# A third addition in chunks 1 to 4, one load moved ahead of another, and a new written order

## The chip, the cores and the metric

The kernel runs on one core of a Trainium2 chip. The metric is device time in microseconds (us). The time before is the median of three runs. A profile is one further execution that the hardware profiler recorded; its times count from the first instruction.

The core has five instruction queues that run side by side: PE (TensorE, matrix multiplication; its weight loads are shown as PEld), DVE (VectorE), ACT (ScalarE), POOL (GpSimd) and SP (SyncE, which here only starts transfers). Each works through its own list in order and waits for others through semaphores. Matmuls write to PSUM, which is used here as eight banks.

## The reference

Linear attention, then a feed-forward layer with SoLU and a layer norm. Cut to what matters:

```python
# q, k, v: (8 batches, 8 heads, 576 rows, 64)
kv  = einsum('bhsd,bhse->bhde', k, v)
o   = einsum('bhsd,bhde->bhse', q, kv)
x   = o / sqrt(mean(o*o, -1) + 1e-6) * g_norm     # then to 4608 rows x 512
h   = x @ w_in                                    # 512 x 1024
e   = exp(h - max(h))
u   = h * e / (sum(e) + 1e-9)                     # over the 1024 columns
ln  = (u - mean(u)) / sqrt(var(u) + 1e-6) * g_ln
out = ln @ w_out                                  # 1024 x 512
```

## The kernel before

The 4608 rows are worked in nine chunks of 512. Chunks 0 to 7 hold 512 of the 576 rows of one batch each; chunk 8 holds the other 64 rows of all eight. Everything between the matmuls lies transposed: features on partitions, the 512 rows of a chunk along the free axis.

The steps of a chunk c, with the names that the order uses (f counts eight groups of 128 features, m four groups of 128 rows, hf two halves of the heads, z the two members of a half):

- `k`, `v`, `q`, `q_last`, `w_in`, `w_out`: loads. They are issued from POOL; all but w_out are turned to bf16 on the way. The second half of chunk 0's k and v is loaded as f32 from SP (`wide`) and converted by `k.0.1` and `v.0.1`. In chunks 0 and 1 each of k, v, q comes in two halves.
- `kv_mm` (line 375): k^T v into PSUM, 72 small matmuls a chunk; `kv`: copies of the result to SBUF, in pieces (line 229).
- `qT`: q transposed, in chunks 0 to 3 by PE (`qT_mm`, line 427) with a copy, from chunk 4 on by a transposing transfer issued from SP.
- `o_mm` (line 448): q times kv. `sq`: squares of o (ACT, line 233). `oa`: the sum of the two squares (line 460). `s_mm` (line 465): the mean over a head. `ln`, `ex`: the inverse root. `x` (line 489): o scaled, on DVE.
- `h` (line 532): x times w_in, four matmuls a group; in chunks 0 to 2 in two parts, the first of which needs only x of the first half and `w_in.0`. `exp` (line 539, ACT) gives e. `u` (line 543, DVE) is h times e; it reads the PSUM bank of h and so sets when that comes free. `usq`: the square of u, on POOL or ACT. `es` (line 551, POOL): e added in pairs of groups, four rows of 512 a chunk.
- `ua.c.l`, `usqa.c.l`, `esa.c.l` (line 575, DVE): folds. Fold l adds the upper half of the groups to the lower, so that eight become four, two, one.
- `sums` (line 594): what the folds left is summed over the partitions by small matmuls, four for each row of 512. `turn`, `stats`, `rstd`: mean, variance and the inverse root.
- `out` (line 651): u times a centred w_out, eight matmuls for 128 rows; in parts of two matmuls in chunk 0, of four in the others. Chunk 8's last tile is done in two halves of 256 columns (line 659). `ob` (lines 239 and 241): the scaling, on DVE or ACT. `store`: two transfers from SP, in chunk 8 one from SP or ACT.
- `w_mean`, `w_center` (lines 632 and 638): the column mean of g_ln times w_out, once, by eight matmuls, and eight DVE instructions that centre w_out. `warm`: matmuls on zeros, as many as `WARM` says; their result is not used.

The sum's denominator and the variance are put together in `stats`; the maximum is not subtracted.

Nothing is scheduled by the compiler. `ORDER` is a list of all these steps, written out; each queue gets its steps in that order. A step runs on its default engine unless a suffix names another (`usq.0.5:act`, `oa.2.1:pool`; `usq` is on POOL, `oa`, `kv`, `ob`, folds are on DVE without a suffix). `ROOMS` names the buffer or PSUM bank that each new tile takes, so a step also waits until the former holder of its room has been read.

`Plan.run` (lines 122 to 139) adds waits beyond those of the data: the next POOL instruction waits for every DVE addition (`ua`, `usqa`, `esa`, `oa`) that stands ahead of it in the order, and POOL loads wait for a transposing transfer ahead of them.

`FOLDS` and `E_FOLDS` give the number of folds of u (and its square) and of e for each chunk. After two folds of u and none of e, `sums` has (2 + 2 + 4) x 4 = 32 matmuls; after three and one, (1 + 1 + 2) x 4 = 16; in chunk 0, without folds, (8 + 8 + 4) x 4 = 80.

Of the kernel before, what the change touches and what calls it, by code (L numbers as in the profile page):

```python
# [25 lines left out]
kv.1.0.0.0 kv.1.0.1.1 kv.1.0.1.0 qT_mm.1.0 ex.0.0 q.2.0 qT.1.0:act x.0.0.0 x.0.0.1 warm.5 o_mm.1.0 sq.1.0.0 warm.6
h.0.6.0 h.0.3.0 k.2.0 sq.1.0.1 x.0.1.0 table h.0.0.0 oa.1.0 x.0.1.1 s_mm.1.0 h.0.2.0 h.0.7.0 h.0.2.1 ln.1.0 v.2.0
ex.1.0 h.0.6.1 x.1.0.1 exp.0.6 q.3.0 h.0.3.1 exp.0.2 x.1.0.0 h.0.7.1 h.0.1.0 exp.0.7 u.0.6 v.3.0 qT_mm.1.1 h.0.0.1
exp.0.3 h.0.1.1 u.0.2 usq.0.6 h.1.2.0 exp.0.0 qT.1.1 kv_mm.1.1.1 exp.0.1 kv_mm.1.1.0 k.3.0 kv.1.1.0.1 h.0.4.0 h.0.4.1
u.0.1 kv.1.1.2.1:act kv.1.1.0.0:act es.0.0 kv.1.1.1.0:act kv.1.1.2.0:act kv.1.1.1.1 u.0.3 o_mm.1.1 exp.0.4 h.0.5.0  # L30
# [10 lines left out]
out.0.3.2 rstd.0 h.2.0.0 ob.0.0:act usq.1.6 kv.3.0.1 ob.0.2 h.2.6.1 kv.3.1.2:act kv.3.0.0:act kv.3.1.1:act out.0.3.3
usqa.1.0 kv.3.0.2:act h.2.4.0 exp.2.6 h.2.5.0 ob.0.3:act ua.1.0 o_mm.3.0 h.2.1.0 store.0.3 sq.3.0.0 h.2.0.1 sq.3.0.1
u.2.6 h.2.1.1 store.0.0 exp.2.0 h.2.5.1 usqa.1.1 out.0.1.0 exp.2.1 oa.3.0 h.2.4.1 ua.1.1 exp.2.5 qT.4 s_mm.3.0
out.0.1.1 u.2.0 ln.3.0 es.1.3 out.0.1.2 u.2.5 h.2.7.0 ex.3.0 h.2.7.1 u.2.1 exp.2.4 es.2.0 h.2.3.0 x.3.0.1 exp.2.7
o_mm.3.1 sq.3.1.0 x.3.0.0 usq.2.6 out.0.1.3 sq.3.1.1 h.2.2.0 h.2.3.1 u.2.7 qT.5 ob.0.1:act h.2.2.1 oa.3.1 sums.1
exp.2.3 u.2.4 es.2.3 kv_mm.4.0 exp.2.2 u.2.3 store.0.1 usq.2.5:act s_mm.3.1 turn.1 es.2.2 out.1.3.0 kv.4.1.0
kv.4.0.1:act ln.3.1 u.2.2 store.0.2 out.1.3.1 kv.4.0.0 usq.2.7 ex.3.1 stats.1 out.1.2.0 kv.4.0.2:act kv.4.1.1 kv.4.1.2
rstd.1 x.3.1.1 usq.2.0 o_mm.4.0 o_mm.4.1 ob.1.3 sq.4.0.1 out.1.0.0 usq.2.4 x.3.1.0 sq.4.0.0 store.1.3 out.1.2.1
sq.4.1.0 oa.4.0 ua.2.0 sq.4.1.1 s_mm.4.0 out.1.0.1 ln.4.0 oa.4.1 h.3.2.0 ex.4.0 ob.1.0 v.5.0 s_mm.4.1 x.4.0.0 h.3.7.0
k.5.0 ln.4.1 x.4.0.1 exp.3.2 es.2.1 h.3.3.0 ex.4.1 u.3.2 h.3.6.0 exp.3.3 ua.2.1 exp.3.7 h.3.5.0 x.4.1.0 u.3.3 v.6.0  # L50
# [685 lines left out]
```

## Time and profile before

| | |
|---|---|
| median of 3 runs | 177.4 us (177.29 to 177.53) |
| the profiled execution: span from the first to the last instruction | 175.8 us |
| its own time beyond the span | not on the page; median less span is 1.6 us |
| PE busy | 164.2 us (93%) |
| ACT busy | 152.1 us (86%) |
| DVE busy | 145.5 us (83%) |
| POOL busy | 99.8 us (57%) |
| chain that ended last | PE 75%, DVE 10%, ACT 5%, DMA 5% |
| granted TensorE clock | 1.000 |

Busy time of PE counts a 128x512 matmul as 379 ns, though a row of them starts one every 0.22 us; they overlap, so short pauses are hidden in it. "Idle before" is the time for which an engine stood still ahead of an instruction, with what ended it. In the chain of waits each step is followed back to what released it, or to the instruction before it on its engine.

### The profile page before, as it was taken

What the parts mean: (1) busy time and instruction counts of PE and PEld (TensorE: products, weight loads), DVE (VectorE), ACT (ScalarE), POOL (GpSimd) and SP (SyncE); (2) the same over time, 40 slices, a digit from 0 to 9 for tenths busy, and PEclk for the clock granted to TensorE, in tenths of its full rate; (3) what the DMA queues carried; (4) which work ended last, traced back from release to release, by engine and by line L of the source; (5) the groups of instructions that cost most, each with busy time, mean ns of one, the idle gap of its engine ahead of it and who ended that gap; (6) DMA issues with size and microseconds to landing.
All of it is one profiled execution on the core that took longest, in us unless ns stands there. A gap on an engine that the chain in (4) does not pass through costs nothing.

```text
span 175.8 us, 4843 instructions
## 1 busy us (share of the span) xinstructions
PE 164.2 (93%) x1913; PEld 80.3 (46%) x1938; DVE 145.5 (83%) x317; ACT 152.1 (86%) x273; POOL 99.8 (57%) x108
## 2 busy tenths in 40 slices
...
GB/s 179 218 203 214 206 275 373 209 208 208 208 210 210 218 210 129 127 206 235 205 183 259 150 52 193 156 73 93 195 206 105 5 118 126 2 60 93 196 213 159
DMA packets 34623, 30.27 MB, mean 172 GB/s; under 512 B 16288, under 2 KB 28328, under 8 KB 34600
## 3 DMA queue, kind: packets, MB, share of 16 engines
...
q10 hardware_dynamic: 432, 0.66, 1.0%
...
HBM read 32.51 MB, written 9.44 MB: 239 GB/s over the span
## 4 chain that ended last, share of the span: by engine, by line
PE 75%; DVE 10%; ACT 5%; DMA 5%; issue 2%; POOL 1%; POOLq 0%; DVEq 0%; ACTq 0%
PE h_ps L532 31%; PE out_ps L651 30%; DMA k_sb<-in_k_dram 5%; PE kv_ps L375 4%; PE o_ps L448 3%; DVE u_sb L543 3%; PE sum_ps L594 3%; PE s_ps L465 3%; DVE x_sb L489 2%; DVE w_out_sb L638 2%; ACT osq_sb L233 2%; DVE osq_sb L460 1%; PE out_ps L659 1%; ACT e_sb L539 1%; ACT kvd L229 1%
## 5 line engine op out<-in xcount | busy, mean ns | idle before, releaser
L532 PE MATMUL h_ps<-x_sb,w_in_sb 128*128 128x512 bf16 x280 | 68.0, 379 | 0.5
L651 PE MATMUL out_ps<-w_out_sb,u_sb 128*128 128x512 bf16 x266 | 65.2, 379 | 0.7 <-issue 0.3
L551 POOL TENSOR_TENSOR es_sb<-e_sb 128x512 bf16<-128x512 f32 x36 | 45.4, 1279 | 33.5 <-ACT e_sb L539 13.0
L539 ACT ACTIVATE e_sb<-h_ps,zero_t 128x512 f32<-128x512 f32 x72 | 46.2, 690 | 2.3 <-PE h_ps L532 1.7
L543 DVE TENSOR_TENSOR u_sb<-h_ps,e_sb 128x512 bf16<-128x512 f32 x72 | 46.6, 684 | 1.3 <-ACT e_sb L539 1.0
L532 PEld LDWEIGHTS <-w_in_sb 128*128 128x128 bf16 x288 | 27.3, 98 | 32.5 <-issue 1.3
L651 PEld LDWEIGHTS <-u_sb 128*128 128x128 bf16 x280 | 26.4, 98 | 31.6 <-issue 1.0
L233 ACT ACTIVATE usq_sb<-u_sb,zero_t 128x512 bf16<-128x512 bf16 x49 | 33.6, 718 | 0.0
L489 DVE SCALAR_TENSOR_TENSOR x_sb<-o_ps,g_sb,rst_sb 128x256 bf16<-128x256 f32 x72 | 30.2, 478 | 3.1 <-ACT rst_sb L476 2.5
L235 POOL TENSOR_TENSOR usq_sb<-u_sb 128x512 bf16<-128x512 bf16 x23 | 23.6, 1043 | 7.9 <-DVE osq_sb L460 5.6
L233 ACT ACTIVATE osq_sb<-o_ps,zero_t 128x512 bf16<-128x512 f32 x36 | 22.8, 689 | 3.5 <-PE o_ps L448 3.4
L239 ACT ACTIVATE ob_sb<-out_ps,rstd 128x512 f32<-128x512 f32 x22 | 14.8, 684 | 4.0 <-PE out_ps L651 3.8
L575 DVE TENSOR_TENSOR usq_sb<-usq_sb 128x2048 bf16<-128x2048 bf16 (+2 forms) x20 | 17.0, 848 | 0.6 <-ACT usq_sb L233 0.4
L229 DVE CAST kvd<-kv_ps 64x128 bf16<-64x128 f32 (+3 forms) x26 | 6.4, 256 | 11.2 <-ACT kvd L229 6.5
L241 DVE TENSOR_SCALAR ob_sb<-out_ps,rstd 128x512 f32<-128x512 f32 (+1 forms) x15 | 10.6, 711 | 4.1 <-PE out_ps L659 2.2
L322 POOL DMA_DIRECT2D v_sb<-in_v_dram x9 | 6.8, 757 | 10.1 <-DVE sum_ps L601 2.8
L472 ACT ACTIVATE lss_sb<-s_ps,eps_t 128x512 f32<-128x512 f32 x16 | 11.1, 695 | 1.0 <-PE s_ps L465 0.7
L476 ACT ACTIVATE rst_sb<-lss_sb,zero_t 128x512 f32<-128x512 f32 x16 | 11.5, 722 | 0.4
L375 PE MATMUL kv_ps<-v_sb,k_sb 64*64 64x64 bf16 x576 | 8.0, 194 | 2.8 <-DMA k_sb<-in_k_dram 1.3
L300 PE MATMUL warm_ps<-zeros 128*128 128x512 bf16 x25 | 8.8, 481 | 1.4 <-DVE zeros L255 1.2
L229 ACT CAST kvd<-kv_ps 64x128 bf16<-64x128 f32 (+3 forms) x34 | 8.2, 243 | 2.2 <-PE kv_ps L375 1.5
L375 PEld LDWEIGHTS <-k_sb 64*64 64x64 bf16 x576 | 6.8, 107 | 6.8 <-DMA k_sb<-in_k_dram 2.6
...
## 6 DMA issues: line engine op xcount, KB each, us to landing
...
k_sb<-in_k_dram POOLq DMA_DIRECT2D x6, 576.0 KB, 13.8
v_sb<-in_v_dram POOLq DMA_DIRECT2D x6, 576.0 KB, 13.0
q_sb<-in_q_dram POOLq DMA_DIRECT2D x6, 512.0 KB, 16.2
...
q_sb<-in_q_dram POOLq DMA_DIRECT2D x4, 256.0 KB, 9.9
w_in_sb<-in_moe_w_in_dram POOLq DMA_DIRECT2D x2, 512.0 KB, 13.4
...
```

The source lines that it names most:

```text
L229: nc.scalar.copy(dst, src) if engine == "act" else on[engine].tensor_copy(dst, src)
L233: nc.scalar.activation(out=dst, in_=src, func=AF.Square, bias=zero_t[:, :])
L235: on[engine].tensor_tensor(out=dst, in0=src, in1=src, op=MUL)
L239: nc.scalar.activation(out=dst, in_=src, func=AF.Copy, scale=by)
L375: nc.tensor.matmul(t[64 * y:64 * y + 64, :], T["k", b][rows, n, i, :], T["v", b][rows, n, i, :], start=(i == 0 and (b < 2 or m == 0)), sto ...
L489: nc.vector.scalar_tensor_tensor(out=t[:, 2 * hf + dh, z], in0=T["o", c, hf, z][:, dh], scalar=g_rep[dh], in1=T["rst", c, hf][:, z], op0=M ...
L532: nc.tensor.matmul(bank(("h", c, f), [128, 512])[:, :], w_in_sb[:, dt, f * 128:(f + 1) * 128], T["x", c][:, dt].rearrange("p a b c -> p (a ...
L539: nc.scalar.activation(out=t[:, f % 2, :], in_=T["h", c, f][:, :], func=AF.Exp, bias=zero_t[:, :])
L543: nc.vector.tensor_tensor(out=t[:, f, :], in0=T["h", c, f][:, :], in1=T["e", c, f // 2][:, f % 2, :], op=MUL)
L551: on[engine].tensor_tensor(out=t[:, n, :], in0=e[:, 0, :], in1=e[:, 1, :], op=ADD)
L575: nc.vector.tensor_tensor(out=to[:, 0:n, :], in0=src[:, 0:n, :], in1=src[:, n:2 * n, :], op=ADD)
L651: nc.tensor.matmul(bank(("out", c, m), [128, d_model])[:, :], T["u", c][:, f, m * 128:(m + 1) * 128], w_out_sb[:, f, :], start=(f == 0), s ...
```

## The change

1. `FOLDS` of chunks 1 to 4 goes from 2 to 3 and `E_FOLDS` from 0 to 1: the new steps are `ua.c.2`, `usqa.c.2` and `esa.c.0` for c from 1 to 4, all on DVE.
2. In POOL's list of loads `w_in.0` stands ahead of `q.1.0`; the order of all other loads is the same.
3. The order of everything else is written anew, with new rooms. Assignments move: on DVE, `ob` falls from 15 to 10, `oa` from 15 to 11, and `v.0.1` is added; on ACT, `ob` rises from 22 to 27 and `usq` falls from 49 to 46; on POOL, `usq` rises from 23 to 26 and `oa` from 1 to 5 (3.0, 4.1, 5.1, 8.0, 8.1 for 2.1). SP gains one store of chunk 8 that ACT had issued, and ACT scales both halves of the last tile.
4. There is an eighth `warm` step, and the warm-up matmuls are 42 instead of 27.

The diff, cut:

```diff
-wide.v ident wide.k g_rows q.0.1 v.0.0 k.0.0 q.0.0 v.0.1:act v.1.0 k.1.0 q.1.0 w_in.0 k.0.1:act w_in.1 warm.0
+ident wide.v v.0.1 wide.k g_rows k.0.1:act warm.0 kv_mm.0.1.1 kv_mm.0.1.0 kv.0.1.1.1:act q.0.1 qT_mm.0.1 qT.0.1:act
+turn_g v.0.0 k.0.0 q.0.0 warm.1 kv_mm.0.0.1 kv.0.0.2.1:act kv_mm.0.0.0 warm.2 qT_mm.0.0 kv.0.1.2.0:act v.1.0 k.1.0
 ...
+o_mm.0.1 w_in.0 q.1.0 qT.0.0 w_in.1 q.1.1 v.1.1 k.1.1 w_out.0 w_out.1 sq.0.1.1 q.2.0 warm.4 o_mm.0.0 sq.0.0.0 sq.0.0.1
 ...
-w_center.4 h.1.0.1 v.4.0 w_center.0 exp.1.7 qT_mm.2.0 exp.1.0 w_center.3 h.1.1.0 h.1.1.1 k.4.0 qT.2.0:act w_center.2
-h.1.2.1 es.0.1 u.1.7 h.1.3.1 exp.1.1 h.1.4.1 u.1.0 exp.1.3 out.0.2.0 es.1.0 usq.0.3 u.1.1 exp.1.2 out.0.2.1 kv_mm.2.0
-w_center.7 exp.1.4 h.1.5.0 w_center.6 kv.2.1.0:act kv.2.0.0:act h.1.5.1 kv.2.0.2:act kv.2.1.1 kv.2.0.1:act es.1.1
-u.1.4 out.0.2.2 kv.2.1.2:act exp.1.5 o_mm.2.0 u.1.3 o_mm.2.1 sq.2.0.1 out.0.2.3 usq.1.1 u.1.2 qT_mm.3.0 sq.2.0.0 u.1.5
-out.0.0.0 sq.2.1.1 oa.2.0 out.0.0.1 sq.2.1.0 qT.3.0 s_mm.2.0 usq.1.5 out.0.0.2 ln.2.0 qT_mm.3.1 oa.2.1:pool ex.2.0
 ...
+v.3.0 kv.1.0.1.0:act kv.1.0.0.0:act table g_mean x.0.0.1 x.0.0.0 kv.1.0.2.1:act warm.6 h.0.0.0 h.0.6.0 x.0.1.1 x.0.1.0
+kv.1.0.2.0 qT_mm.1.0 qT.1.0 h.0.3.0 h.0.4.0 o_mm.1.0 h.0.1.0 h.0.4.1 sq.1.0.0 h.0.1.1 sq.1.0.1 oa.1.0 h.0.6.1 exp.0.4
 ...
+h.0.2.0 exp.0.5 u.0.5 es.0.0 q.4.0 es.0.3 q.5.0 h.0.2.1 exp.0.2 es.0.1 es.0.2 w_mean.0 u.0.7 u.0.2 v.4.0 w_mean.1 k.4.0
+w_mean.2 w_mean.3 s_mm.1.1 ln.1.1 usq.0.6 ex.1.1 x.1.1.0 x.1.1.1 usq.0.7:act usq.0.0:act usq.0.2:act h.1.2.0 h.1.4.0
 ...
+h.1.7.1 qT_mm.2.0 exp.1.6 u.1.6 qT.2.0:act es.1.2 usq.1.0 sums.0 exp.1.7 u.1.7 kv_mm.2.0 kv.2.0.0:act kv.2.1.1:act
+turn.0 out.0.1.0 out.0.2.0 out.0.2.1 kv.2.0.1:act kv.2.1.2:act kv.2.0.2:act kv.2.1.0:act o_mm.2.0 usq.1.5:act
+w_center.6 stats.0 o_mm.2.1 w_center.7 out.0.1.1 out.0.1.2 sq.2.0.0 sq.2.0.1 oa.2.0 out.0.0.0 out.0.0.1 ua.1.0 sq.2.1.0
+sq.2.1.1 oa.2.1 s_mm.2.0 ln.2.0 es.1.1 out.0.1.3 out.0.2.2 out.0.2.3 out.0.0.2 out.0.0.3 s_mm.2.1 rstd.0 ex.2.0 ob.0.1
 ...
+es.3.0 usq.3.0 ua.3.0 sq.5.1.0 oa.5.1:pool exp.4.0 u.4.2 u.4.0 h.4.5.0 exp.4.5 sq.5.0.1 u.4.5 out.2.3.0 out.2.3.1
 ...
+stats.8 out.8.1.0 out.8.1.1 rstd.8 ob.8.0 ob.8.2:act store.7.1 store.8.2:act out.8.3.0 ob.8.3.0:act ob.8.1 store.8.0
+store.8.1 store.8.3.0 out.8.3.1 ob.8.3.1:act store.8.3.1:act
 ...
-14 3 1 3 1 4 1
+17 9 2 1 1 6 5 1
 ...
-    FOLDS = (0, 2, 2, 2, 2, 3, 3, 3, 3)
-    E_FOLDS = (0, 0, 0, 0, 0, 1, 1, 1, 1)
+    FOLDS = (0, 3, 3, 3, 3, 3, 3, 3, 3)
+    E_FOLDS = (0, 1, 1, 1, 1, 1, 1, 1, 1)
```

126 lines of the change are left out of this document (59 added, 67 removed).

## The prediction

> **What bounds the kernel now.** I read the page's head, then busy time by stretch, to find where PE (TensorE's matmul queue) is not full, then the timeline and the chain of waits in those places.
>
> ```profile
> span 175.8 us, 4843 instructions
> ...
> PE 164.2 (93%) x1913; PEld 80.3 (46%) x1938; DVE 145.5 (83%) x317; ACT 152.1 (86%) x273; POOL 99.8 (57%) x108
> ```
>
> The span is 175.8 us; the median of the runs shown is 177.4, so 1.6 us lie around the span. The page gives no other time of this execution, and I carry the 1.6 us unchanged: the sum is made on the span and added to 177.4.
>
> Busy time by stretch (columns: stretch, PE, PEld, DVE, ACT, POOL, granted clock, DMA share, GB/s):
>
> ```profile
> 20.00:30.00 10.00, 9.81 (x96) 4.66 (x96) 7.75 (x17) 9.61 (x18) 6.54 (x8) 1.00 1.21 305
> 30.00:45.00 15.00, 13.04 (x172) 7.17 (x174) 14.10 (x26) 13.75 (x26) 12.77 (x14) 1.00 1.22 211
> 45.00:50.00 5.00, 4.98 (x171) 3.25 (x171) 4.11 (x12) 4.51 (x8) 5.00 (x5) 1.00 1.23 207
> 50.00:160.00 110.00, 109.00 (x1189) 51.55 (x1204) 104.78 (x214) 105.58 (x192) 63.29 (x61) 1.00 0.80 146
> ```
>
> From 45 us on PE stands still for 1.0 us in 115, spread thin: there only less PE work, or a new wait, moves the end. Between 20 and 45 us it idles 0.19 + 1.96 = 2.15 us; this can be won back. ACT has 4.4 us free in the long stretch and DVE 5.2. The clock is 1.00 throughout, so more warm-up matmuls win no speed.
>
> The start, in the timeline and in the DMA issues with their time to landing:
>
> ```profile
> 6.07 0.75 POOL L322 DMA_DIRECT2D q_sb<-in_q_dram  x1
> 6.78 0.61 POOL L343 DMA_DIRECT2D w_in_sb<-in_moe_w_in_dram  x1
> 8.41 0.54 POOL L343 DMA_DIRECT2D w_in_sb<-in_moe_w_in_dram  x1 [1.03 <-DMA q_sb<-in_q_dram]
> ...
> 22.79 0.74 POOL L322 DMA_DIRECT2D v_sb<-in_v_dram  x1 [1.98 <-DMA w_in_sb<-in_moe_w_in_dram]
> ```
> ```profile
> 19.83 0.98 PEld L532 LDWEIGHTS <-w_in_sb 128*128 128x128 bf16 x6 [0.27 <-DMA w_in_sb<-in_moe_w_in_dram]
> ```
> ```profile
> w_in_sb<-in_moe_w_in_dram POOLq DMA_DIRECT2D x1, 512.0 KB, 13.0
> q_sb<-in_q_dram POOLq DMA_DIRECT2D x1, 256.0 KB, 11.3
> ```
> ```profile
> w_in_sb<-in_moe_w_in_dram POOLq DMA_DIRECT2D x1, 512.0 KB, 13.8
> ```
> ```profile
> v_sb<-in_v_dram POOLq DMA_DIRECT2D x1, 576.0 KB, 17.5
> ```
>
> Issue plus time to landing: q.1.0 is there at 17.4, w_in.0 at 19.8, w_in.1 at 22.2, chunk 2's v at 40.3. The loads arrive one behind the other, and the first h (line 532) waits for w_in.0.
>
> ```profile
> 26.60 0.76 PE L375 MATMUL kv_ps<-v_sb,k_sb 64*64 64x64 bf16 x36
> ...
> 31.08 0.38 PE L465 MATMUL s_ps<-osq_sb,head_mean 128*128 128x512 bf16 x1 [0.71 <-DVE osq_sb L460]
> 31.10 1.95 PE L632 MATMUL mean_ps<-u_sb,ua_sb 128*128 128x512 f32 x7
> ...
> 40.40 0.77 PE L375 MATMUL kv_ps<-v_sb,k_sb 64*64 64x64 bf16 x72 [0.51 <-DVE u_sb L543]
> ...
> 42.50 0.72 PE L448 MATMUL o_ps<-qT_sb,kvd 64*32 64x256 bf16 x32
> ...
> 44.92 0.38 PE L465 MATMUL s_ps<-osq_sb,head_mean 128*128 128x512 bf16 x1
> ```
>
> Three marks for later: kv_mm.2.0 starts at 40.40, o_mm.2.0 at 42.50, s_mm.2.0 at 44.92. No order can start kv_mm.2.0 before its v lands at 40.3.
>
> **The change part by part.** Prices of PE's pieces, from the chain of waits:
>
> ```profile
> 47.86 1.30 PE sum_ps L594 x80
> ...
> 61.53 0.56 PE sum_ps L594 x32
> ...
> 93.89 3.45 PE h_ps L532 x16
> ...
> 130.04 0.34 PE sum_ps L594 x16
> ```
>
> *Third folds.* In chunks 1 to 4 u and its square are added down to one row each instead of two, and e to two instead of four: sums has 16 small matmuls where it had 32, 0.34 for 0.56 us, four times: **-0.88 us** of PE work, all behind 45 us where PE is full. Without that cover it would be worth nothing.
>
> *What pays for it*, by shapes (count | busy us, mean ns of one | idle before, releaser):
>
> ```profile
> L233 ACT ACTIVATE usq_sb<-u_sb,zero_t 128x512 bf16<-128x512 bf16 x49 | 33.6, 718 | 0.0
> ...
> L235 POOL TENSOR_TENSOR usq_sb<-u_sb 128x512 bf16<-128x512 bf16 x23 | 23.6, 1043 | 7.9 <-DVE osq_sb L460 5.6 <-DVE usq_sb L575 2.2
> L233 ACT ACTIVATE osq_sb<-o_ps,zero_t 128x512 bf16<-128x512 f32 x36 | 22.8, 689 | 3.5 <-PE o_ps L448 3.4
> L239 ACT ACTIVATE ob_sb<-out_ps,rstd 128x512 f32<-128x512 f32 x22 | 14.8, 684 | 4.0 <-PE out_ps L651 3.8
> ...
> L241 DVE TENSOR_SCALAR ob_sb<-out_ps,rstd 128x512 f32<-128x512 f32 x13 | 9.6, 747 | 1.9 <-ACT rstd L617 1.0 <-PE out_ps L651 0.9
> ...
> L460 DVE TENSOR_TENSOR osq_sb<-osq_sb 128x512 bf16<-128x512 bf16 x15 | 6.7, 445 | 1.0 <-ACT osq_sb L233 0.6
> ...
> L575 DVE TENSOR_TENSOR es_sb<-es_sb 128x1024 bf16<-128x1024 bf16 x4 | 2.7, 685 | 0.0
> ...
> L229 ACT CAST kvd<-kv_ps 128x128 bf16<-128x128 f32 x8 | 2.0, 265 | 1.0 <-PE kv_ps L375 0.9
> ...
> L575 DVE TENSOR_TENSOR usq_sb<-usq_sb 128x512 bf16<-128x512 bf16 x4 | 1.7, 423 | 0.0
> L575 DVE TENSOR_TENSOR ua_sb<-ua_sb 128x512 bf16<-128x512 bf16 x4 | 1.7, 419 | 0.0
> ...
> L460 POOL TENSOR_TENSOR osq_sb<-osq_sb 128x512 bf16<-128x512 bf16 x1 | 1.1, 1150 | 0.0
> ```
>
> DVE gains 4 x (0.42 + 0.42 + 0.69) = 6.1 us and gives away four o additions (1.8) and five scalings (three whole ones 2.2, two halves under 1.5): about +1 us against 5.2 free. ACT takes those scalings (3 x 0.68, two halves at most as much) for three squares fewer (0.72 each): at most +1.3 us, taken as 1, against 4.4 free. POOL gets three squares (3.1) and four o additions (4.6), +7.7 us in a span where it works 57%. The conversion of v.0.1 moves from ACT to DVE in the first 8 us, while k.0.1's, which lands later, stays: 0. On average none becomes the bound: 0 us, from 0 up to the second rival. Plan.run makes the next POOL instruction wait for every DVE addition ahead of it in the order, so twelve folds are twelve such waits; behind them stand es and the loads of chunks 5 to 7. The order leaves 12.0 us of PE work between v.5.0 and its use (9.7 before), so I price them at 0; without that cover a late load stops PE for its whole delay.
>
> *The swap of w_in.0 and q.1.0.* w_in.0's turn lasted 2.4 us (17.4 to 19.8) and q.1.0 has half its bytes, so w_in.0 lands 1.2 to 2.4 us earlier, at 17.4 to 18.6, and q.1.0 near 19.8. The first h then waits for its x and five warm-up matmuls, somewhere from there to the old 19.8; I take 18.9. qT_mm.1.0 stands behind two h now, which hide the later q. But w_in.1 lands at 22.2 as before, and ahead of it both orders have issued ten h matmuls; before also had chunk 1's s_mm behind it, 0.2 us. Alone: **0 us**, bounds -0.9 (the earlier first h survives) and +0.5 (qT_mm.1.0 waits for q). Every other load keeps its place in POOL's queue, and SP's queue only gains one late store.
>
> *Warm-up matmuls.* 42 for 27; fourteen of the fifteen more stand before the first h, in waits for k and x; warm.7 is one h-sized matmul, 3.45 / 16 = 0.22 us, in front of a load, so 0 to 0.22, contained in the walk below.
>
> *The new order from 22.3 to 46 us*: the largest term. PE's list from h.0.4.1 to kv_mm.2.0 is 54 h matmuls (11.7 us), 8 w_mean (1.95 / 7 each: 2.2), three q transposes (about 0.5 each, between a kv group and its neighbours: 1.6), two 18-matmul kv groups (0.7), one o_mm (0.4), two s_mm (0.5), warm.7 and sums.0 (1.3): 18.6 us, so 40.9 without a wait. Waits I find by setting each piece against what it needs: kv_mm.1.1.0 not before 26.6 (its group started there; PE comes at 26.3), h.1.6.0 for the PSUM bank that ln.1.1 frees (0.1), crumbs 0.1. So **kv_mm.2.0 at 41.4, 1.0 us later** than before. But behind it 3.05 us less work is left: h.1.5 and h.1.6 (8 matmuls, 1.73) and sums.0 (1.30) moved ahead of it, the first two parts of out.0.2 (4 matmuls, 0.86) behind it, and the 0.88 of the folds. The w_center stall (0.51 for u in the row above) and the 0.71 at s_mm.1.1 do not return: s_mm.1.1 now stands behind h.0.2 and four w_mean.
>
> Late next is the copying of kv.2, all six pieces on ACT: 41.4 + 0.8 + 6 x 0.265 = 43.8, which puts o_mm.2.0 at 43.9 (PE is through with out.0.1.0 and out.0.2.0-1 at 43.6), and s_mm.2.0, behind o_mm.2 (0.72) and eight out matmuls (1.73), at 46.4, 1.5 later than before, with 3.03 us less PE work left. Sum at that mark: 1.48 - 3.03 = **-1.55 us**. The bounds of this term: kv_mm.2.0 right after its load and everything behind as before, -3.0; all 2.15 us of idle lost again, +0.6.
>
> *The tail.* The last half of the last tile is scaled on ACT instead of DVE and stored from the same queue; 0 us, plus or minus 0.2. sums.8 has 9.8 us of PE work between the last h and itself, 12.4 before; ACT and DVE work far below full there. 0, up to +1.
>
> The sum: 177.4 - 1.55 = **175.9 us**. It assumes that PE stays as full behind 46 us as before.
>
> **A rule against the change.** First the rows:
>
> ```profile
> 71.30 1.29 POOL L551 TENSOR_TENSOR es_sb<-e_sb 128x512 bf16<-128x512 f32 x1
> ...
> 72.29 0.85 DVE L575 TENSOR_TENSOR ua_sb<-ua_sb 128x1024 bf16<-128x1024 bf16 x1
> ```
>
> One fold began inside a POOL addition and ended 0.27 us behind it, in 0.85 us. The Trainium skill's page "SBUF — State Buffer", section "Who interferes with whom", says that a VectorE instruction with two SBUF inputs and a GpSimd instruction reading SBUF exclude each other for a whole instruction. By that rule each of twelve new folds may wait for what is left of a POOL addition; here that would have held this fold for up to 0.3 us. Its row agrees in part: 0.17 us above the 0.685 of the same shape.
>
> **The rivals.**
> 1. *PE is even better filled*: kv_mm.2.0 starts when its load lands. For: 2.15 us of idle are there, and all work before 40 us is free of that load. Against: my walk has 18.6 us of work in 18.1. 177.4 - 3.05, about 174.4.
> 2. *Slower: additions of o on POOL hold up s_mm.* One 1.15 us instruction for 0.445, behind whatever POOL is doing. From the order PE has 2.9 us of work from the second square to s_mm.5.1, 3.5 at chunk 8's two, 5.1 at chunks 3 and 4. Two squares (0.69 each), the addition and one POOL addition before it (1.29) are 3.8: waits of 0.9 and twice 0.3; with a POOL square (1.04) in front as well 2.0 and twice 1.4. Against: before, oa.2.1 ran on POOL unnoticed. At the upper price 175.9 + 4.8 = 180.7; halfway 179.0. It makes the kernel slower from 1.9 us in all, 0.6 at each of those three.
> 3. *No gain in the end*: PE asks 1.5 us earlier, but ACT and DVE, about 1 us fuller each, cannot deliver; 1.5 us are handed back in many small waits. For: 4.4 and 5.2 us of freedom shrink by 1 + 1.55 each. Against: they stay above 1.8. 177.4.
> 4. *Folds and POOL exclude each other*: a fold held for half a POOL addition, twelve times 0.64 = 7.7 us on DVE against 4 free: 175.9 + 3.7 = 179.6. The fold of 0.85 us speaks weakly for it.
>
> **How the numbers follow.** Forecast 0.56, rival 1 0.10, rival 2 0.14, rival 3 0.16, rival 4 0.04. The likeliest case alone spans 175.1 to 176.9 (a walk without its waits and crumbs below; half a microsecond of new waits and a late sums.8 above). The range reaches into rivals 1 and 3 and the light end of 2: 174.8 to 177.9. A measurement here tells 0.2% (0.35 us) from no change: faster 0.66, within 0.16, slower 0.18.
>
> **What would show it.** Right: the sums groups of chunks 1 to 4 as x16 at 0.34 us; first h near 18.9 without a gain at w_in.1; kv_mm.2.0 at 41.4, o_mm.2.0 at 43.9, s_mm.2.0 at 46.4; PE idle from 30 to 45 us about 1 us instead of 1.96; at most 1.2 us idle from 50 to 160. Wrong: s_mm waiting for POOL's osq in chunks 5 and 8 (rival 2); e or u ending many waits behind 50 us (3); folds of 128x512 far above 0.42 us (4); or kv_mm.2.0 at 43.4 instead of 41.4, which leaves nothing of the 3.05.

## The result and the profile after

| | before | after |
|---|---|---|
| median | 177.37 us (177.29 to 177.53) | 178.38 us (178.19 to 178.6) |
| after / before | | 1.0055, 95% interval 1.0041 to 1.0069 |
| span of the profiled execution | 175.8 us | 176.4 us (whole execution 178.19) |

The changed kernel is half a per cent slower; 175.9 had been forecast. In every later comparison the time beyond the span has a median of 1.8 us for the old and the new kernels alike, so the difference lies inside the span. The two profiled executions are 0.6 us apart, the medians 1.0: what is read from the two traces accounts for 0.6.

The page of the kernel after, its head and its chain by engine:

```profile
span 176.4 us, 4777 instructions
...
PE 166.4 (94%) x1864; PEld 80.8 (46%) x1889; DVE 148.8 (84%) x322; ACT 149.9 (85%) x273; POOL 107.5 (61%) x115
...
ACT 33%; PE 30%; DVE 25%; DMA 5%; issue 5%; SPq 0%; ACTq 0%; DVEq 0%
```

The chain that ended last was PE for 75% before. Now ACT and DVE hold 58% of it: PE does 0.9 us less of sums and yet ends later, because it waits for them in the places below.

Busy time by stretch (stretch, PE, PEld, DVE, ACT, POOL, clock, DMA share, GB/s), after:

```profile
30.00:45.00 15.00, 14.58 (x249) 8.51 (x250) 14.88 (x30) 14.63 (x28) 13.25 (x14) 1.00 1.22 210
...
50.00:100.00 50.00, 48.76 (x641) 22.95 (x649) 48.68 (x104) 48.88 (x91) 34.71 (x33) 1.00 0.98 189
100.00:150.00 50.00, 48.96 (x481) 22.64 (x486) 47.48 (x96) 47.45 (x85) 31.34 (x31) 1.00 0.72 122
```

The same view of the kernel before:

```profile
50.00:100.00 50.00, 49.47 (x629) 23.42 (x637) 48.10 (x99) 48.70 (x93) 31.25 (x30) 1.00 1.04 196
100.00:150.00 50.00, 49.63 (x504) 23.67 (x508) 46.79 (x97) 47.23 (x84) 27.84 (x28) 1.00 0.69 120
```

From 30 to 45 us PE's idle time fell from 1.96 to 0.42 us, as wanted. From 50 to 150 us it rose from 0.90 to 2.28. That is the result in two stretches.

The marks of the prediction, in the timeline of the kernel after:

```profile
19.82 1.02 PE L532 MATMUL h_ps<-x_sb,w_in_sb 128*128 128x512 bf16 x3
...
42.08 0.78 PE L375 MATMUL kv_ps<-v_sb,k_sb 64*64 64x64 bf16 x72
44.38 0.65 PE L448 MATMUL o_ps<-qT_sb,kvd 64*32 64x256 bf16 x32
46.69 0.38 PE L465 MATMUL s_ps<-osq_sb,head_mean 128*128 128x512 bf16 x1
...
115.93 0.24 PE L594 MATMUL sum_ps<-ua_sb,stat_sel 128*32 128x128 bf16 x4
115.99 0.23 PE L594 MATMUL sum_ps<-usq_sb,stat_sel 128*32 128x128 bf16 x4
116.05 0.28 PE L594 MATMUL sum_ps<-es_sb,stat_sel 128*32 128x128 bf16 x8
```

**How the loss is followed.** For each piece of PE I add its start and all PE work that stands from there to the end of the list, without waits: 0.216 us for a matmul of h, out or s_mm, 0.71 for a whole kv_mm, 0.57 for both halves of o_mm, 0.34 or 0.56 for sums, and so on, the same prices for every kernel. I call the sum the projected end. It stays level while PE is full and rises by each wait (and by about 0.15 us where PE changes from one kind of matmul to another). At s_mm.2.0 it is 44.92 + 125.09 = 170.0 before and 46.69 + 122.06 = 168.8 after. Each row below is one profiled execution, which can lie off its kernel's median: e1's took 178.95 us, e8's 182.5, e12's 179.1, the changed kernel's 178.19. Differences in the text are taken before rounding. All kernels of this study, in us:

| kernel | s_mm.2.0 | kv_mm.4.0 | o_mm.4.0 | kv_mm.6.0 | kv_mm.7.0 | o_mm.8.0 | last group |
|---|---|---|---|---|---|---|---|
| before | 170.0 | 170.8 | 170.9 | 171.5 | 171.9 | 172.1 | 172.4 |
| after | 168.8 | 169.6 | 170.3 | 170.9 | 171.4 | 172.6 | 173.0 |
| e1 folds back | 169.5 | 170.1 | 170.8 | 172.0 | 173.2 | 173.4 | 173.7 |
| e2 folds alone | 169.2 | 171.4 | 171.7 | 174.2 | 175.9 | 177.4 | 177.8 |
| e3 swap alone | 172.2 | 172.8 | 172.9 | 173.6 | 173.9 | 174.1 | 174.5 |
| e4 o additions back | 168.7 | 170.2 | 170.9 | 172.8 | 173.4 | 174.6 | 175.2 |
| e5 new start, old rest | 169.5 | 173.1 | 173.6 | 174.7 | 175.2 | 175.4 | 175.8 |
| e6 new to 59 us, old rest | 169.2 | 171.2 | 174.4 | 175.0 | 175.4 | 175.6 | 176.0 |
| e7 old start, new rest | 169.1 | 172.1 | 172.7 | 173.3 | 174.0 | 175.0 | 176.1 |
| e8 three steps moved | 168.9 | 169.7 | 169.8 | 171.0 | 171.5 | 176.6 | 176.9 |
| e9 ob.1.0 on ACT | 168.9 | 169.7 | 169.8 | 170.9 | 171.5 | 172.7 | 173.1 |
| e10 kv.7 later | 168.6 | 169.5 | 170.2 | 170.8 | 171.4 | 172.6 | 173.0 |
| e11 both | 168.6 | 169.5 | 169.6 | 170.7 | 171.3 | 172.5 | 172.9 |
| e12 chunk 4's folds back | 168.8 | 169.6 | 170.4 | 171.0 | 171.5 | 172.7 | 173.2 |
| e13 two folds freed | 168.8 | 169.6 | 169.7 | 170.9 | 171.3 | 172.3 | 172.7 |
| e14 swap back | 168.7 | 169.5 | 170.3 | 170.9 | 171.4 | 172.7 | 173.0 |
| e15 POOL additions alone | 169.9 | 171.8 | 172.0 | 174.6 | 174.9 | 175.1 | 175.9 |
| e16 short warm-up | 168.7 | 169.5 | 170.3 | 170.9 | 171.4 | 172.7 | 173.2 |
| e17 ob.4.3 early | 168.7 | 169.5 | 169.7 | 170.9 | 171.4 | 172.3 | 173.5 |
| e18 all | 168.5 | 169.4 | 169.5 | 171.1 | 171.5 | 172.3 | 173.5 |

The changed kernel is 1.25 us ahead at s_mm.2.0 and 0.6 behind at the end: it gains 1.25 and then loses 4.2 where the kernel before lost 2.4. The two largest single losses are at o_mm.4.0 (0.74, at 67.5 us) and at out.4.1.0 (0.59, at 121); the rest is in pieces of 0.1 to 0.3. (A larger one seems to follow at out.4.3.0, but there the record of the first matmul is missing from the trace: 15 of 16 are listed.) Its waits of PE in these places:

```profile
PE o_ps L448 <- DVE kvd L229: 0.6, 1, 0.6
...
PE out_ps L651 <- ACT ob_sb L239: 0.4, 1, 0.4
```

### The profile page after: what moved, and what is told of

Read it like the earlier page. It is cut to its first block, busy times and chain, and to the rows that moved or that the text cites. A ratio compares the mean times of both kernels' runs of the same rounds, so it can differ in the third digit from the quotient of the medians.

```text
span 176.4 us, 4777 instructions
## 1 busy us (share of the span) xinstructions
PE 166.4 (94%) x1864; PEld 80.8 (46%) x1889; DVE 148.8 (84%) x322; ACT 149.9 (85%) x273; POOL 107.5 (61%) x115
## 4 chain that ended last, share of the span: by engine, by line
ACT 33%; PE 30%; DVE 25%; DMA 5%; issue 5%; SPq 0%; ACTq 0%; DVEq 0%
PE h_ps L532 11%; PE out_ps L651 8%; ACT e_sb L539 8%; DVE u_sb L543 7%; ACT usq_sb L233 5%; ACT osq_sb L233 5%; DVE x_sb L489 4%; ACT ob_sb L239 4%; DVE ua_sb L575 3%; DVE usq_sb L575 3%; DMA u_sb<-in_k_dram 3%; ACT kvd L229 3%; ACT lss_sb L472 3%; DVE kvd L229 2%; PE kv_ps L375 2%
## 5 line engine op out<-in xcount | busy, mean ns | idle before, releaser
L543 DVE TENSOR_TENSOR u_sb<-h_ps,e_sb 128x512 bf16<-128x512 f32 x72 | 46.1, 681 | 1.5 <-ACT e_sb L539 1.3
L235 POOL TENSOR_TENSOR usq_sb<-u_sb 128x512 bf16<-128x512 bf16 x26 | 26.9, 1045 | 12.6 <-DVE osq_sb L460 6.6
L233 ACT ACTIVATE usq_sb<-u_sb,zero_t 128x512 bf16<-128x512 bf16 x46 | 31.7, 724 | 0.4 <-DVE u_sb L543 0.4
L239 ACT ACTIVATE ob_sb<-out_ps,rstd 128x512 f32<-128x512 f32 (+1 forms) x27 | 17.8, 672 | 3.4 <-DMA out_dram<-ob_sb 2.5
L575 DVE TENSOR_TENSOR usq_sb<-usq_sb 128x2048 bf16<-128x2048 bf16 (+2 forms) x24 | 19.0, 790 | 0.5 <-ACT usq_sb L233 0.4
L300 PE MATMUL warm_ps<-zeros 128*128 128x512 bf16 x40 | 11.5, 421 | 1.5 <-DVE zeros L255 1.2
L229 ACT CAST kvd<-kv_ps 64x128 bf16<-64x128 f32 (+3 forms) x33 | 7.5, 240 | 5.4 <-PE kv_ps L375 2.8
L322 POOL DMA_DIRECT2D q_sb<-in_q_dram x10 | 7.7, 766 | 5.9 <-PE kv_ps L375 2.2
L575 DVE TENSOR_TENSOR ua_sb<-u_sb 128x2048 bf16<-128x2048 bf16 x8 | 9.9, 1238 | 0.0
L575 DVE TENSOR_TENSOR ua_sb<-ua_sb 128x1024 bf16<-128x1024 bf16 (+1 forms) x16 | 9.8, 613 | 0.1
```

What stands on the lines that cost most here:

```text
L229: nc.scalar.copy(dst, src) if engine == "act" else on[engine].tensor_copy(dst, src)
L233: nc.scalar.activation(out=dst, in_=src, func=AF.Square, bias=zero_t[:, :])
L235: on[engine].tensor_tensor(out=dst, in0=src, in1=src, op=MUL)
L239: nc.scalar.activation(out=dst, in_=src, func=AF.Copy, scale=by)
L543: nc.vector.tensor_tensor(out=t[:, f, :], in0=T["h", c, f][:, :], in1=T["e", c, f // 2][:, f % 2, :], op=MUL)
L575: nc.vector.tensor_tensor(out=to[:, 0:n, :], in0=src[:, 0:n, :], in1=src[:, n:2 * n, :], op=ADD)
```

## The experiments

The theories named in the expectations: **A**, the new order's later part has waits of its own, which hand the gain back; **B**, the start leaves ACT and DVE a backlog that falls due in any order; **C**, ACT and DVE are so full that each wait removed returns at the next step; **D**, DVE's long folds beside POOL make the loss. Times are medians; the ratio to the kernel before, measured on the same chip in the same hour, has its 95% interval behind it.

### The parts, each alone and each taken back

**e1, all twelve folds taken back from the changed kernel.**

```diff
-    FOLDS = (0, 3, 3, 3, 3, 3, 3, 3, 3)
-    E_FOLDS = (0, 1, 1, 1, 1, 1, 1, 1, 1)
+    FOLDS = (0, 2, 2, 2, 2, 3, 3, 3, 3)
+    E_FOLDS = (0, 0, 0, 0, 0, 1, 1, 1, 1)
 # and ua.c.2, usqa.c.2, esa.c.0 for c = 1 to 4 out of ORDER
```

> The new order without its third folds (FOLDS 2 and E_FOLDS 0 in chunks 1 to 4, the twelve DVE steps taken out). Theory A, the folds fill DVE where it is already full (54 to 67 us, and the stretch from 107 to 125): the 0.88 us of PE work comes back, but about 2 us of waits go: 177.0 to 177.6, ratio to before 0.998 to 1.001. Theory B, the loss sits in the new order itself and the folds are a gain there: 179.0 to 179.5, ratio 1.009 to 1.012.

178.66 us, 1.0055 (1.0037 to 1.0073): the same as with them. PE has 0.88 us more work, DVE about 6 us less, and the end does not move. The table shows where the difference went: from kv_mm.7.0 to o_mm.8.0 only 0.2 is lost instead of 1.2, but 1.1 from o_mm.4.0 to kv_mm.6.0 and 1.2 from there to kv_mm.7.0, where the changed kernel loses 0.6 and 0.5.

**e2, the folds alone, in the order before** (`ua.c.2` behind `ua.c.1`, `usqa.c.2` behind `usqa.c.1`, `esa.c.0` right ahead of `sums.c`).

```diff
-... usqa.2.0 usqa.2.1 exp.4.6 ob.1.1:act u.4.7 kv_mm.5.0 usq.3.5 exp.3.0 u.3.1 sums.2 ...
+... usqa.2.0 usqa.2.1 usqa.2.2 exp.4.6 ob.1.1:act u.4.7 kv_mm.5.0 usq.3.5 exp.3.0 u.3.1 esa.2.0 sums.2 ...
```

> The kernel before with only the third folds added, each right behind the second one, esa ahead of sums. Theory A (folds fill DVE): between 177.3 and 178.5, no gain, with DVE-released waits of PE in chunks 2 to 5. Theory B (the folds are worth their 0.88 us of PE work): 176.4 to 176.8, ratio 0.995 to 0.997.

183.03 us, 1.0309 (1.0271 to 1.0346). The folds that cost nothing in the new order cost 5.4 us in the old one, put in at these places and with no other step moved. The waits of PE in that kernel begin with the added fold itself, right ahead of the sums that need it:

```profile
PE sum_ps L595 <- DVE es_sb L576: 4.1, 4, 1.6
```

**e3, the swap alone, in the order before.**

```diff
-v.1.0 k.1.0 q.1.0 w_in.0 k.0.1:act w_in.1
+v.1.0 k.1.0 w_in.0 q.1.0 k.0.1:act w_in.1
```

> The kernel before with only w_in.0 issued ahead of q.1.0. In its order qT_mm.1.0 and o_mm.1.0 stand ahead of the first h, so q.1.0, landing at 19.4 to 19.8, holds up the first h by about 1 to 2 us; w_in.1 still lands near 22. Both theories: 177.4 to 178.4, no gain. A theory in which w_in.0 is what limits the start expects a gain of 0.5 us or more, 176.9.

179.75 us, 1.0128 (1.0099 to 1.0156). The old order asks for qT_mm.1.0 ahead of the first h, and PE stands for the q that now comes last:

```profile
PE qt_ps L427 <- DMA q_sb<-in_q_dram: 2.8, 1, 2.8
```

**e14, the swap taken back in the changed kernel.**

```diff
-o_mm.0.1 w_in.0 q.1.0 qT.0.0 w_in.1 q.1.1
+o_mm.0.1 q.1.0 w_in.0 qT.0.0 w_in.1 q.1.1
```

> The changed kernel with the swap alone undone: q.1.0 asked for ahead of w_in.0, nothing else. In the changed kernel the first h stood at 19.82 us, behind w_in.0's landing at 18.07, and qT_mm.1.0 behind q.1.0 at 19.36. If the new order was fitted to the swap: w_in.0 lands 1.3 to 2 us later, about 19.8, the first h with it, and the end by 0.3 to 2 us later, 178.7 to 180.4. If the swap is of no account in this order: 178.4.

178.32 us, 1.0048 (1.0029 to 1.0068): no difference to the changed kernel. The first h starts at 19.78 us instead of 19.82. In the new order neither load is what it waits for (see e16).

**e4, the five o additions taken back from POOL to DVE in the changed kernel; e15, the same five put on POOL in the order before.**

```diff
 # e4
-oa.3.0:pool  oa.4.1:pool  oa.5.1:pool  oa.8.0:pool  oa.8.1:pool
+oa.3.0  oa.4.1  oa.5.1  oa.8.0  oa.8.1
 # e15, in the order before
-oa.3.0  oa.4.1  oa.5.1  oa.8.0  oa.8.1
+oa.3.0:pool  oa.4.1:pool  oa.5.1:pool  oa.8.0:pool  oa.8.1:pool
```

> The new order with the five additions of squares of o back on DVE at the same places. Theory C (the prediction's second rival: POOL's additions hold up s_mm): faster than the change by 0.5 us or more, 177.9 or less. Theories A and B: PE never waited for a POOL addition in the trace of the change, and DVE gets 5 x 0.44 us more: 178.4 to 179.0, ratio 1.006 to 1.009.

> The kernel before with one part of the change alone: the same five additions of o (oa.3.0, .4.1, .5.1, .8.0, .8.1) on POOL. In the changed kernel they save 2.0 us (180.42 without). If they help as DVE's relief anywhere: 175.5 to 177. If the order before has no place for them, as it had none for the folds (+5.4 us) or the swap (+2.2): 178 to 181.

e4: 180.42 us, 1.0157 (1.0142 to 1.0173), 2.0 us more than the changed kernel by the medians and 1.8 by the two ratios: on POOL these additions are a gain there. e15 (oa.2.1 stays on POOL too): 181.11 us, 1.0201 (1.0178 to 1.0223), 3.5 us more than the kernel before. In the waits of PE of e15, and in its timeline, stands the second rival of the prediction in the flesh:

```profile
PE s_ps L465 <- POOL osq_sb L460: 2.8, 3, 1.3
```
```profile
86.50 1.96 POOL L460 TENSOR_TENSOR osq_sb<-osq_sb 128x512 bf16<-128x512 bf16 x1 [0.36 <-ACT osq_sb L233]
```
```profile
88.51 0.38 PE L465 MATMUL s_ps<-osq_sb,head_mean 128*128 128x512 bf16 x1 [1.33 <-POOL osq_sb L460]
```

The addition took 1.96 us there, for 1.15 in most other places, and PE stood 1.33 us for it. It had begun 0.27 us into a fold of DVE (ua.3.0, from 86.23 us, 1.21 us long), so 0.94 us of that fold were left, and it took 0.81 us more: here the fourth rival's mechanism, which the prediction feared for DVE's folds, lengthens the second's. In the changed kernel no s_mm waits for POOL. So of each part the same holds: free or a gain in the order made with it, 2.1 to 5.4 us in the other.

### Half of one order, half of the other

The steps that are left are taken in the other order; a room whose former holder is not yet done is replaced by a free one.

```diff
 # e5: ORDER of after up to x.2.0.0 (48 us), then the rest of before; folds of before
 # e6: ORDER of after up to sums.1 (59 us), then the rest of before; chunk 1 folded as after
 # e7: ORDER and WARM of before up to x.2.0.1 (49 us), then the rest of after; folds of after
```

> The new order up to x.2.0.0 (about 48 us), then every step that is left in the order of the kernel before, with its folds (twice in chunks 1 to 4). Theory A (the new order's later part hands the time back, in waits of its own): at s_mm.2.0 PE stands at 46.69 us with 122.94 us of matmul work left, 169.6, against 44.92 + 125.09 = 170.0 in the kernel before; the rest then loses the 2.4 us that it lost there, so 0.4 us faster than before, 177.0, up to 0.8 more if the seam costs a wait. Theory B (the new start puts PE ahead by leaving ACT and DVE work behind, which falls due later in any order): 178 or above, the same loss as in the changed kernel.

> The new order up to sums.1 (about 59 us, chunk 1 folded three times), then the order of the kernel before with its folds for chunks 2 to 4. At sums.1 the changed kernel's PE stood at 58.56 us; with 111.33 us of work left in this kernel that is 169.9, against 170.8 in the kernel before. Theory A: 0.9 us faster than before, 176.5, with the seam up to 177.3. Theory B: 178 or above.

> The order of the kernel before up to x.2.0.1 (about 49 us), with its warm-up matmuls, then every step that is left in the new order, folded three times. At s_mm.2.0 this is 44.92 + 124.21 = 169.1. Theory A: the new rest then loses its 4.2 us as in the changed kernel, 173.3 for the last matmul against 172.4 before, so 0.9 us slower than before, 178.3. Theory B: the rest loses less without the backlog, about 3 us, so 177.0 or below.

Measured: 181.05 (1.0199, 1.0184 to 1.0214), 181.41 (1.0225, 1.0203 to 1.0247) and 180.77 us (1.0183, 1.0166 to 1.0201). A's expectations missed in all three, B's in e7; e5 and e6 lie inside B's "178 or above", but not by its cause: from s_mm.2.0 to o_mm.4.0, across the seam, the three lose 3.7 to 5.2 us, where the whole kernels lose 0.9 and 1.5. In e6 about 1.7 of the 5.2 is not a wait at all: from 64.2 to 67.6 us, behind waits of 0.85, 0.17 and 1.09 us, the granted clock was 0.50, and in all five executions its mean over the span was 0.99. So as totals the three do not tell A from B. The waits of PE in e5 show the seam, x arriving late at a PE that has changed lists:

```profile
PE kv_ps L375 <- DVE x_sb L489: 1.6, 1, 1.6
...
PE h_ps L532 <- DVE x_sb L489: 1.1, 1, 1.1
```

Behind the seam the table does tell something. From o_mm.4.0 to the last group the old rest loses 1.5 us in the kernel before, 1.5 in e3, 1.6 in e6 and 2.2 in e5; the new rest loses 2.6 in the kernel after, 2.7 in e14 and 3.3 in e7. The loss goes with the order of that stretch and hardly with what came ahead of it, and in e1, the new order without the folds, it is 2.9. Of these e7 speaks most for A: with the old start and a long stand at the seam the new rest still loses 3.3. The old rest of e5 and e6 says less against B, because ACT and DVE could work off a backlog while PE stood at the seam.

### Taking single waits away from the changed kernel

The place of the 0.74 us, in DVE's and PE's timeline of the kernel after:

```profile
64.33 1.39 DVE L229 CAST kvd<-kv_ps 64x128 bf16<-64x128 f32 x5
65.75 0.75 DVE L241 TENSOR_SCALAR ob_sb<-out_ps,rstd 128x512 f32<-128x512 f32 x1
66.42 0.68 DVE L543 TENSOR_TENSOR u_sb<-h_ps,e_sb 128x512 bf16<-128x512 f32 x1
67.13 0.29 DVE L229 CAST kvd<-kv_ps 64x128 bf16<-64x128 f32 x1
```
```profile
67.48 0.65 PE L448 MATMUL o_ps<-qT_sb,kvd 64*32 64x256 bf16 x32 [0.58 <-DVE kvd L229]
```

Five of six copies of kv.4 are made, then ob.1.0 and u.2.0, then the sixth copy, on which o_mm.4.0 waits. Two folds, from the timeline of the kernel after; the same shape takes 0.685 us elsewhere:

```profile
110.73 1.72 DVE L575 TENSOR_TENSOR ua_sb<-ua_sb 128x1024 bf16<-128x1024 bf16 x1
...
119.12 1.53 DVE L575 TENSOR_TENSOR es_sb<-es_sb 128x1024 bf16<-128x1024 bf16 x1
```

Beside them on POOL:

```profile
110.55 1.34 POOL L551 TENSOR_TENSOR es_sb<-e_sb 128x512 bf16<-128x512 f32 x1
...
118.79 2.31 POOL L338 DMA_DIRECT2D q_last<-in_q_dram  x3
```

**e8, three steps moved.**

```diff
-kv.4.0.1 kv.4.0.2 ob.1.0 u.2.0 usq.2.4 es.2.0 usq.2.7 out.1.1.0 kv.4.1.1 o_mm.4.0
+kv.4.0.1 kv.4.0.2 kv.4.1.1 ob.1.0 u.2.0 usq.2.4 es.2.0 usq.2.7 out.1.1.0 o_mm.4.0
-ua.4.0 es.5.3 rstd.3 ... ua.4.1 ua.4.2
+ua.4.0 rstd.3 ... ua.4.1 ua.4.2 es.5.3
-usq.5.3 store.3.1 q_last.6 q_last.2 q_last.5 kv.7.0.0:act ... ob.3.2:act esa.5.0
+usq.5.3 store.3.1 kv.7.0.0:act ... ob.3.2:act esa.5.0 q_last.6 q_last.2 q_last.5
```

> The changed kernel with three steps moved: kv.4.1.1 ahead of ob.1.0 and u.2.0 on DVE (o_mm.4.0 waited 0.65 us for it at 66.8), POOL's es.5.3 behind ua.4.2 (ua.4.1 took 1.72 instead of 0.68 us beside it), and POOL's loads q_last.6, .2, .5 behind esa.5.0 (it took 1.53 instead of 0.69 us beside them). Theory A with these places as its causes: 0.65 us at o_mm.4.0 and up to 1 us by 124 us, 176.7 to 177.7. Rival: DVE and ACT are full there and another wait takes the place of each, 178.4 (178.2 to 178.7).

180.93 us, 1.0213 (1.0177 to 1.0249). At o_mm.4.0 the first matmul starts as hoped and the other 31 do not:

```profile
66.94 0.28 PE L449 MATMUL o_ps<-qT_sb,kvd 64*32 64x256 bf16 x1
67.58 0.65 PE L449 MATMUL o_ps<-qT_sb,kvd 64*32 64x256 bf16 x31 [0.36 <-DVE u_sb L544]
```

The second bank of o_mm.4.0 was held by h.2.0, which u.2.0 reads: two waits lay on one place, 0.3 us apart (u.2.0 ended at 67.10 us in the kernel after, the last copy at 67.42). From there the projected end is where it was in the changed kernel, up to 121 us. The 2.5 us that e8 loses come behind that, by the trace from the three loads q_last, 2.7 us later: they now run beside six stores of SP, ACT's ob.4.0 waits 2.42 us for one of these to leave its buffer, and PE's s_mm.7.1 for ACT; SP's transposition of chunk 8's q waits for the loads and starts at 129.53 instead of 125.33 us, with the next stores behind it. POOL's issue, SP's queue, ACT's row and the wait of PE:

```profile
121.50 2.31 POOL L339 DMA_DIRECT2D q_last<-in_q_dram  x3 [0.22 <-DVE u_sb L544]
```
```profile
121.32 3.67 SPq L680 DMA_DIRECT2D out_dram<-ob_sb  x6
129.53 1.63 SPq L436 DMA_TRANSPOSE qT_sb<-q_last  x1
```
```profile
128.91 0.69 ACT L240 ACTIVATE ob_sb<-out_ps,rstd 128x512 f32<-128x512 f32 x1 [2.42 <-DMA out_dram<-ob_sb]
```
```profile
PE s_ps L466 <- ACT ob_sb L240: 2.3, 1, 2.3
```

The profiled execution lost more, 3.9 us at the last group. Behind the wait of 2.29 us at 129.65 the granted clock was 0.50 from 130.0 to 133.4 us, and the eight matmuls of out at 129.87 took 3.49 us where eight take 1.89 at full clock: about 1.7 us more. The page's row of the clock, in 40 slices, shows it:

```profile
PEclk9999999999999999999999999999879999999999
```

This is no rule: in e5 PE stood 1.6 us for x, and the clock stayed at 1.00.

**e9, e10, e11: DVE relieved at 67 us; ACT's idle 1.33 us at 117 filled; both.**

```diff
 # e9
-exp.2.0 usq.2.1:act out.1.3.0 s_mm.3.1 ln.3.1 ... kv.4.0.2 ob.1.0 u.2.0 ... kv.4.1.1 o_mm.4.0 sq.4.0.0 sq.4.0.1
+exp.2.0 out.1.3.0 s_mm.3.1 ob.1.0:act ln.3.1 ... kv.4.0.2 kv.4.1.1 u.2.0 ... o_mm.4.0 sq.4.0.0 sq.4.0.1 usq.2.1:act
 # e10
-kv.7.0.0:act kv.7.1.0:act exp.6.7 h.6.3.0 exp.6.3
+kv.7.0.0:act exp.6.7 h.6.3.0 exp.6.3 kv.7.1.0:act
 # e11: both
```

> The changed kernel with the place at 67 us relieved on DVE: ob.1.0 (0.75 us) goes to ACT ahead of ln.3.1, kv.4.1.1 goes behind kv.4.0.2, and ACT's usq.2.1 moves into ACT's idle 0.61 us behind sq.4.0.1. o_mm.4.0 then starts at 66.85 instead of 67.48. Theory A (the loss sits in single places of the new order, and what one gives back is kept to the end): 0.6 us less, 177.8. Rival C (ACT and DVE are so full behind it that the wait comes again within 20 us): 178.4, with the projected end after o_mm.5.0 as in the changed kernel, 170.4 to 170.9.

> The changed kernel with one ACT step moved: kv.7.1.0 behind exp.6.7 and exp.6.3. ACT stood idle for 1.33 us at 117 us ahead of it, behind two copies that DVE made of the same PSUM tile. Theory A: ob.3.2 is about 1 us earlier, out.4.1.0 (121.37) no longer waits for its bank, 0.6 to 0.9 us less, 177.5 to 177.8. Rival C: DVE's u.6.7 to u.6.6 and the folds behind them set the place, 178.2 to 178.5.

> Both edits together. Theory A: the gains add, 1.2 to 1.5 us less than the changed kernel, 176.9 to 177.2, at or below the kernel before. Rival C: 178.2 to 178.5.

178.53 (1.0057, 1.0042 to 1.0072), 178.52 (1.0056, 1.0038 to 1.0074) and 178.38 us (1.0048, 1.0032 to 1.0064): C in all three. e9 starts o_mm.4.0 at 66.92, its projected end there is 0.55 us better, and at kv_mm.5.0 (80.1 us) 170.4 for 170.4: the gain is gone in 13 us, in waits of 0.2 at h.3.6.0 and 0.3 at h.3.3.0. e10 wins 0.46 at out.4.1.0 and gives 0.42 of it back within 3 us. In e11's timeline o_mm.7.0 now waits for a u of DVE:

```profile
123.38 0.43 PE L449 MATMUL o_ps<-qT_sb,kvd 64*32 64x256 bf16 x16 [0.17 <-DVE u_sb L544]
```

**e12, only chunk 4's three folds taken back.**

```diff
-    FOLDS = (0, 3, 3, 3, 3, 3, 3, 3, 3)
-    E_FOLDS = (0, 1, 1, 1, 1, 1, 1, 1, 1)
+    FOLDS = (0, 3, 3, 3, 2, 3, 3, 3, 3)
+    E_FOLDS = (0, 1, 1, 1, 0, 1, 1, 1, 1)
```

> The changed kernel with the three added folds of chunk 4 alone taken back (0.42 + 0.42 + 0.68 us of DVE and the 1.04 us by which a POOL addition held ua.4.1 are at stake, sums.4 gets 0.22 us longer). If the folds of chunk 4 cause the loss of 1 us between 115 and 124 us: 0.8 us less, 177.6. If they only use up what was idle (as all twelve did in the kernel with the folds taken back, 178.66): 178.4 to 178.7.

178.35 us, 1.0056 (1.0033 to 1.008), a wide spread (177.44 to 179.66). In the profiled execution, which took 179.1, the 0.7 us that it saves by 124 us comes back as a wait of 0.74 at s_mm.7.1, for ACT's ob. The long fold of chunk 4 is still there (1.73 us), so the added folds are not what held it.

**e13, the two long folds freed, on top of e11.**

```diff
-q_last.0 q_last.4 ua.4.0 es.5.3 rstd.3 ob.3.3:act usqa.4.0 ex.6.1
+ua.4.0 rstd.3 ob.3.3:act usqa.4.0 es.5.3 q_last.0 q_last.4 ex.6.1
-ob.3.2:act esa.5.0 h.6.6.0 ... u.6.6 o_mm.7.1 ua.5.0
+ob.3.2:act h.6.6.0 ... u.6.6 esa.5.0 o_mm.7.1 ua.5.0
```

> The kernel with both edits (e11), and the two long folds freed: esa.5.0 (1.52 instead of 0.68 us) goes behind u.6.6, after POOL's loads are issued, and POOL's es.5.3 goes ahead of the loads q_last.0 and q_last.4, beside DVE's products x.6.1, so that ua.4.1 (1.72 instead of 0.68 us) starts after it. DVE gets 1.9 us back between 110 and 124 us. Theory D (DVE, back to back there, sets the pace, and the two held folds make the loss at 115 to 124 us): 0.8 to 1.2 us less than that kernel, 177.2 to 177.6, about the kernel before. Rival C (every place freed is handed back to the next wait): 178.2 to 178.5.

178.01 us, 1.0029 (1.0015 to 1.0042): the best of the new order, 0.37 us below e11, less than half of what D wanted and a little more than C allowed (178.2). Both folds are short, and PE gains 0.5 us to s_mm.7.0 (projected end 171.8 for 172.35 in e11). Then out.5.0.0 stands for ob.4.3, the next step of DVE, and takes 0.44 back (the row counts 0.27 of it as idle, since a matmul counts as busy beyond the start of the next):

```profile
110.68 1.14 DVE L576 TENSOR_TENSOR ua_sb<-ua_sb 128x1024 bf16<-128x1024 bf16 x2
...
123.05 0.68 DVE L576 TENSOR_TENSOR es_sb<-es_sb 128x1024 bf16<-128x1024 bf16 x1
```
```profile
129.26 1.89 PE L652 MATMUL out_ps<-w_out_sb,u_sb 128*128 128x512 bf16 x8 [0.27 <-DVE ob_sb L242]
```

**e16, a short warm.6; e17, ob.4.3 early, on top of e13; e18, all of it.**

```diff
 # e16
-17 9 2 1 1 6 5 1
+17 9 2 1 1 6 2 1
 # e17
-usqa.5.1 ... ua.5.2 ... usqa.5.2 oa.7.0 usq.6.5 ... s_mm.7.0 ob.4.3
+usqa.5.1 ... oa.7.0 ob.4.3 ua.5.2 usqa.5.2 usq.6.5 ... s_mm.7.0
 # e18: e17 with the WARM of e16
```

> The changed kernel with warm.6, right ahead of the first h, 2 matmuls long instead of 5 (0.65 us less). In the changed kernel warm.6 ran from 18.55 to 19.82 us, while w_in.0 had landed at 18.07 and DVE's first x stood at about 19.0. Start-bound: the first h at 19.2, 0.6 us earlier, and 0.3 to 0.6 us less at the end, 177.8 to 178.1. Rival C (the later waits take up what the start gains): 178.3 to 178.5. Against both: if the longer warm-up kept the granted clock up, a clock under 1.0 and a later end.

> The kernel with the two holds freed (e13) and DVE's ob.4.3 ahead of ua.5.2 and usqa.5.2: out.5.0.0 waited 0.44 us for it at 129.3. Theory D (behind 115 us DVE's own order sets the pace): 177.5 to 177.7, level with the kernel before. Rival C: 178.0.

> All of these together: ob.1.0 on ACT, kv.7.1.0 behind the exponentials, the two folds freed, ob.4.3 early, warm.6 short. If the gains add: 176.9 to 177.3, faster than both kernels by 0.2 to 0.4%. If rival C takes the start's gain: 177.5 to 178.0.

178.81 (1.0082, 1.0063 to 1.0101), 178.70 (1.0077, 1.0059 to 1.0096) and 179.0 us (1.0091, 1.0069 to 1.0113). All expectations missed. In e16 PE waits where the warm-up stood, for DVE's x; the first h starts at 19.76:

```profile
PE h_ps L532 <- DVE x_sb L489: 0.7, 1, 0.7
```

In e17 the wait of out.5.0.0 is gone. DVE's folds are 0.7 us later, POOL's next instruction waits for them by the rule of the order, and POOL is still behind at 136 us:

```profile
129.47 1.04 POOL L236 TENSOR_TENSOR usq_sb<-u_sb 128x512 bf16<-128x512 bf16 x1 [7.33 <-DVE usq_sb L576]
...
135.16 1.16 POOL L461 TENSOR_TENSOR osq_sb<-osq_sb 128x512 bf16<-128x512 bf16 x1
```
```profile
136.37 0.38 PE L466 MATMUL s_ps<-osq_sb,head_mean 128*128 128x512 bf16 x1 [0.77 <-POOL osq_sb L461]
```

No version beats the kernel before.

## Why the prediction was wrong, step by step

- **The failed step is the last sentence of the sum**: that PE stays as full behind 46 us as before. It lost 4.2 us there (projected end 168.8 to 173.0), the kernel before 2.4. This is the third rival, ACT and DVE handing the gain back in waits, with a size that was not foreseen: I let it return 1.5 us, it returned 1.8 of a gain of 1.25. Its argument against ("they stay above 1.8 us free") took a mean over 110 us, and that mean came out better than feared: from 50 to 160 us DVE is busy 105.72 us for 104.78 before (+0.9, about 1 forecast), ACT 105.68 for 105.58 (+0.1, 1 forecast), and yet PE stands 2.33 us there for the "at most 1.2". The waits sit in places where DVE runs back to back, as in the rows from 64.33 to 67.13 us. The sign named for this rival did not appear: no e or u stands in the list of PE's waits behind 50 us; copies of kv and ob end the largest.
- **Third folds, -0.88 us at no cost**: the PE work went as said (16 matmuls, 0.34 us), its worth did not. e1 puts it at nothing: DVE's 6 us cost nothing at the end, and PE's 0.88 us turned into waiting. "0 on average" was right for DVE's busy time and said nothing on the order: e2 paid 5.4 us for the same folds.
- **The swap, 0**: right in the new order (e14), for another reason than given. The first h came at 19.82, not 18.9, because DVE finished its x then (e16), not because of w_in.0 or the warm-up. In the old order the swap costs 2.1 us (e3).
- **Warm-ups, 0 to 0.22**: warm.7, which this term prices, was taken out in no run. e16, with warm.6 0.65 us shorter, gained nothing; the clock of its profile stayed at 1.00.
- **The walk of the new order, -1.55 at s_mm.2.0**: right in kind, 0.3 too good. kv_mm.2.0 came at 42.08 for 41.4, o_mm.2.0 at 44.38 for 43.9, s_mm.2.0 at 46.69 for 46.4; PE's idle time from 30 to 45 us was 0.42 us for the forecast 1. The first h was 0.9 us late, kv_mm.2.0 0.7. (In the list of pieces "warm.7 and sums.0 (1.3)" should read 1.5, 0.22 + 1.30; the total of 18.6 has it right.)
- **The tail, 0**: right. From the start of the last group to the end of the last scaling pass 2.4 us in both kernels.
- **Rival 2, POOL's o additions**: did not happen in the changed kernel, where they are worth about 2 us (e4). Its mechanism and its size are real in an order that was not made for it: e15 shows 2.8 us of such waits, and e17 made one of 0.77.
- **Rival 4, folds and POOL exclude each other**: two long folds cost DVE 1.9 us, 2.7 with the small holds over the whole span, against 0.65 in the kernel before and 7.7 in the rival. (For the second of the two no POOL addition stands beside it; see below.) Freeing the two brought 0.37 us (e13, intervals overlapping e11's).

**What stays open.** 0.5 us of the loss against the kernel before remains in e13, spread over waits of 0.1 to 0.4 us. That the new later part as a whole is worse by about 1.1 us from o_mm.4.0 on is shown by the table, one execution for each kernel; which of its choices does it is not. That repairs in it brought nothing at the end was seen in seven kernels (e8 to e12, e17, e18); in e9 to e12 and in e17 the traces show the time lost again at a later step.
